# Values loaded between head pairs 1 and 2 in the first unit of a sparse attention and gated FFN kernel

## The chip, the core and the metric

The kernel runs on one core of a Trainium2 chip. The metric is the device time of one execution in microseconds; lower is better. The engines are named as in the profile: PE is TensorE (matmuls), PEld its weight loads, DVE is VectorE, ACT is ScalarE, POOL is GpSimd, and SP is SyncE, which here only issues DMAs. PSUM is the memory that PE writes[...].

## What is computed

The attention sees, for each query, a band of nearby keys (a distance below 16) and one entry for each block of 32 keys: the elementwise maximum of the block's keys, and the mean of its values. A gated FFN with a residual follows. Cut to what matters, the reference is:

```python
B, H, S, D = q.shape                         # 4, 8, 768, 64
block, window = (32, 16)
k_sum = k.reshape(B, H, nb, block, D).max(axis=3)
v_sum = v.reshape(B, H, nb, block, D).mean(axis=3)
scores_l = scale * np.matmul(q, k.transpose(0, 1, 3, 2))
mask_l = np.abs(pos[:, None] - pos[None, :]) < window
scores_s = scale * np.einsum('bhsd,bhnd->bhsn', q, k_sum) + np.log(block)
a = softmax(concat([where(mask_l, scores_l, -1e9), scores_s]))
attn = a @ concat([v, v_sum])                # then (B*S, H*D) = (3072, 512)

g = x @ w_gate                               # 512 x 1536
gelu = 0.5 * g * (1.0 + erf(g * inv_sqrt2))
ffn_out = gelu * (x @ w_val) @ w_out         # 1536 x 512
res_gate = 1.0 / (1.0 + np.exp(-(x @ w_res)))
return x + res_gate * ffn_out
```

## The kernel before

**Tiling.** The work is cut into 8 units (`NU`): unit u is half (384 queries, `TU`) of batch u // 2. Inside a unit the heads go in four pairs (`NP`), two heads of 64 dimensions filling 128 partitions. The queries are taken in tiles of 64 (`QT`). For each tile, `kW` holds 128 key columns: 96 of the band (the tile's own 64 and 16 on either side) and 24 block maxima, the rest zero. So one matmul (`s_step`, L330) gives both kinds of score. ACT takes the exponential into `P` (L336, L339). `av_part` multiplies `P` by `vext`, which holds the band's values in rows 0 to 95, and by the block means in rows 96 to 127, which for unit 0 come from a tile of their own, `vsum`. A column of ones gives the softmax's denominator. `av_norm` divides (L370, L372), and `xt_step` transposes the result into `xT` (L381 on PE, L383 on ACT).

**The FFN.** For each of 12 column groups of 128 (`FO`), `fo_step` multiplies `xT` by `w_gate` and by `w_val`, four matmuls each over the head pairs (`half_fo`, L398). ACT applies Gelu and DVE the product. `ffn_step` multiplies by `w_out` (L432), `res_step` by `w_res`, and `end_step` stores.

**What sets the order.** There is one order, written out by hand (`tc.manual_schedule()`): each engine runs its instructions in the order in which the code names them. Buffers come from pools, and an instruction waits until its inputs are there and its buffer is free. In PSUM, `MM` has four banks that are handed out in turn, `AO` and `TT` one bank each, and `SS` two.

**The loads.** All the casting loads are issued by POOL in one queue: first k and q of head pair 1 (heads 2, 3; `load_tokens`, L91), then those of pairs 2 and 3, then the values (`load_values`, L100; seven transfers, of which c = 6 and c = 0 come first), then the weights in six column slices, with the second half of q (`qb`) ahead of the last slice, `w_res` and `w_out`. k and q of pair 0 come as fp32 through SP. Between these issues POOL builds constants with `select` (L119): the identity `ident`, the mask `maskt`, the bias, and `bmean`, the matrix with 1/32 in each block's place that sums values to block means on PE.

**The first unit**, before the loop over units, goes:
- `k_first(hp)`: 16 transposes of k on PE (L226), and ACT's copy into `kW` (L228); `k_first_rest`: DVE's block maximum from the same PSUM tile (L234) and three copies (L236 to L238); `q_step`: the same for q (L195, L219).
- For each pair `mask_into` writes the mask into PSUM ahead of the scores (L313), so that the scores need no mask after it. `s_step` follows.
- `vsum_sum` (L279) sums the value blocks over seven matmuls into `vs`; `vsum_out` (L284) copies them to `vsum`. `v_spread` (L291, L294) copies values inside `vext` for the odd tiles.
- `av_part` runs in two halves: `blocks=False` for the band, `blocks=True` for the block means.
- `keep_warm(n)` issues n matmuls on a constant tile (L449). A Gelu on one element (L504) brings the Gelu table load ahead of the FFN.
- `firsts` holds the four PSUM tiles of FFN columns 0 and 1, into which each pair's projection goes as soon as its `xT` is there.

In the order before, all four pairs' scores are issued ahead of the band part of `av_part`. The second half's q, `qb`, is transposed inside unit 0's FFN loop (L596 to L598), behind columns 9 and 10; after the loop come the next unit's scores, `s_step(n, 0)` and `s_step(n, 1)`, the latter writing to `AO` and `TT`.

Of the kernel before, what the change touches and what calls it, by code (L numbers as in the profile page):

```python
# [8 lines left out]
F32 = mybir.dt.float32  # L9
BF16 = mybir.dt.bfloat16  # L10
AF = mybir.ActivationFunctionType
ALU = mybir.AluOpType
# [3 lines left out]
def kernel(  # L16
# [11 lines left out]
    nc = tc.nc  # L28
    B, H, S, D = q.shape
    assert (B, H, S, D) == (4, 8, 768, 64)  # L30
    BLK, WIN = 32, 16
# [57 lines left out]
    def load_tokens(t, src, b, lo, hi, h0, h1):  # L89
        j = (hi - lo) // PP  # L90
        nc.gpsimd.dma_start(  # L91
            out=t[:, h0:h1].rearrange("p h j d -> p h (j d)"),
            in_=src[b, h0:h1, lo:hi].rearrange("h (p j) d -> p h (j d)", j=j),
        )
# [9 lines left out]
    with tc.manual_schedule():  # L104
# [13 lines left out]
        def select(ap, op, fill, base, step, cm):  # L118
            nc.gpsimd.affine_select(out=ap, in_=ap, compare_op=op, fill=fill, base=base,  # L119
                                    pattern=[[step, ap.shape[-1]]], channel_multiplier=cm)  # L120

        nc.vector.memset(warm[:], 0.0)
        nc.vector.memset(ident[:], 0.0)
        nc.vector.memset(bias_t[:], 0.0)
        nc.vector.memset(bias_t[96:128, :], logblk)
        nc.vector.memset(bmean[:], 1.0 / BLK)
        nc.vector.memset(maskt[:], 1.0)
        vext_consts(0)
        kw_consts(0)
        nc.vector.memset(vsum[0][96:128, :, D:D + 1], 1.0)  # L130
# [7 lines left out]
        load_tokens(kt, k, 0, 0, S, 2, 4)  # L138
        select(ident[:], ALU.not_equal, 1.0, 0, -1, 1)
        load_tokens(qa, q, 0, 0, TU, 2, 4)  # L140
        for h in (4, 6):
            load_tokens(kt, k, 0, 0, S, h, h + 2)
            load_tokens(qa, q, 0, 0, TU, h, h + 2)
        select(maskt[0:96], ALU.is_ge, 0.0, -1, -1, 1)
        select(maskt[0:96], ALU.is_ge, 0.0, 2 * WIN - 1, 1, -1)
        load_values(0, NC)
# [1 line left out]
        select(bias_t[96:128, :], ALU.is_ge, -30000.0, NB - 1, 0, -1)  # L148
        for c in range(1, NC):
            load_values(0, c)  # L150
        select(bmean[:], ALU.is_ge, 0.0, 32 * (NB + 94) - WIN, -32, 1)
        select(bmean[:], ALU.is_ge, 0.0, 31 + WIN - 32 * (NB + 94), 32, -1)

        wg_src = moe_w_gate.rearrange("(ko ki) f -> ki ko f", ki=128)
        wv_src = moe_w_val.rearrange("(ko ki) f -> ki ko f", ki=128)
        for c in range(6):
            sl = slice(c * 256, (c + 1) * 256)
            if c == 5:
                load_tokens(qb, q, 0, TU, S, 0, H)
            nc.gpsimd.dma_start(out=w_gate[:, :, sl], in_=wg_src[:, :, sl])  # L160
            nc.gpsimd.dma_start(out=w_val[:, :, sl], in_=wv_src[:, :, sl])
        nc.gpsimd.dma_start(out=w_res[:], in_=moe_w_res.rearrange("(ko ki) f -> ki ko f", ki=128))
        wo_src = moe_w_out.rearrange("(fo ki) f -> ki fo f", ki=128)
        for c in range(3):
# [52 lines left out]
        def q_step(src, b, lo, hi, hp, pool, tag, copy=nc.scalar.copy):  # L217
            tp = turn_pair(src, hp, pool, tag)
            copy(qT[b % 2][hp][:, lo:hi].rearrange("d (p j) -> d p j", j=tp.shape[2]), tp)  # L219
# [12 lines left out]
        def k_first_rest(tp, kw):  # L232
            ks = work.tile([128, NB], BF16, tag="ks", name="ks")
            nc.vector.tensor_reduce(out=ks[:], in_=tp.rearrange("d j (n w) -> d n j w", w=4),  # L234
                                    axis=mybir.AxisListType.XY, op=ALU.max)
            nc.vector.tensor_copy(kw[:, 0:HT, BLK0:BLK0 + NB], ks.unsqueeze(1).to_broadcast([128, HT, NB]))  # L236
            nc.vector.tensor_copy(kw[:, 1:HT, 0:WIN], kw[:, 0:HT - 1, OWN + QT - WIN:OWN + QT])
            nc.vector.tensor_copy(kw[:, 0:HT, POST:POST + WIN], kw[:, 1:HT + 1, OWN:OWN + WIN])  # L238
# [44 lines left out]
        def vsum_out(b, vs, h0, h1, copy):  # L283
            copy(vsum[b % 2][96:128, h0:h1, 0:D],  # L284
                 vs[96:128, h0 * D:h1 * D].rearrange("p (h d) -> p h d", d=D))

        def v_spread(b, c0, c1, part):

# [190 lines left out]
        k_first_rest(*t)  # L479
        t = k_first(1)  # L480
        q_step(qa, 0, 0, TU, 1, *MM)
        k_first_rest(*t)
        s = mask_into(s_tiles())
        keep_warm(2, s1[0])
        s_step(0, 0, st, s)
        keep_warm(2, s1[0])
        mask_into(s1)
        t = k_first(2)
        q_step(qa, 0, 0, TU, 2, *MM)
        k_first_rest(*t)  # L490
        s_step(0, 1, st, s1, True)
        s = mask_into(s_tiles())
        t = k_first(3)
        q_step(qa, 0, 0, TU, 3, *MM, nc.vector.tensor_copy)
        k_first_rest(*t)
        vs = ps_mm.tile([128, DM], F32, tag="mm", name="vs")
        keep_warm(1, vs)
        s_step(0, 2, st, s)
        s3 = mask_into(s_tiles((AO, TT)))
        wp = ps_mm.tile([128, 512], F32, tag="mm", name="wp")  # L500
        vsum_sum(0, *MM, (NC, 0), vs)
        keep_warm(2, wp)
        s_step(0, 3, st, s3, True)
        nc.scalar.activation(pre[:], bias_t[0:1, :], AF.Gelu)  # L504
        v_spread(0, 0, HT // 2, 0)
        v_spread(0, 0, HT // 2, 1)
        vsum_sum(0, *MM, (1, 2, 3), vs, first=False)
        keep_warm(2, wp)
        homes = (MM, MM, AO, TT)
        for hp in range(2):  # L510
            av_part(0, hp, st, *homes[hp], blocks=False)
        vsum_sum(0, *MM, (4,), vs, first=False)
        for hp in range(2, NP):
            av_part(0, hp, st, *homes[hp], blocks=False)
        keep_warm(1, wp)
        vsum_sum(0, *MM, (5,), vs, first=False, last=True)
        keep_warm(1, wp)
        vsum_out(0, vs, 0, 2, nc.vector.tensor_copy)
        vsum_out(0, vs, 2, 8, nc.scalar.copy)
        for hp in range(NP):  # L520
            av_part(0, hp, st, blocks=True)
            av_norm(hp, st)
        two = ps_s.tile([128, 2, 512], F32, tag="s", name="gv0")
        firsts = [(w_gate, 0, two[:, 0, :]), (w_val, 0, two[:, 1, :]), (w_gate, 1, None), (w_val, 1, None)]
        for hp in range(NP):
            xt_step(0, hp, st, *(MM, MM, AO, TT)[hp], nc.scalar.copy)
            if hp == 0:
                keep_warm(2, wp)
            if hp:
                firsts = [(w, fo, half_fo(st, w, fo, hp - 1, hp, acc)) for w, fo, acc in firsts]  # L530

        for u in range(NU):
            b, half = u // 2, u % 2
# [16 lines left out]
            for fo in range(FO):  # L550
                if u == 0 and fo < 2:
                    for w, _, acc in firsts[2 * fo:2 * fo + 2]:
                        half_fo(st, w, fo, KO - 1, KO, acc)
                    fo_end(gvT, fo, firsts[2 * fo][2], firsts[2 * fo + 1][2])
                elif u > 3 and fo == 0:
                    fo_end(gvT, fo, firsts[0][2], firsts[1][2])
                elif u > 3 and fo == 1:
                    fo_end(gvT, fo, firsts[2][2], half_fo(st, w_val, fo, 0, KO))
                else:
                    fo_step(st, gvT, fo)  # L560
                values_step(u, fo)
                if u == 0 and fo == 4:
                    nc.vector.memset(vsT[:], 0.0)
                    load_rows(1)
                if u == 0 and fo == 6:
                    vext_consts(1)
                if u == 0 and fo == FO - 1:
                    kw_consts(1)
                    for c in range(NC + 1):
                        load_values(1, c)  # L570
                if u == 2 and fo == FO - 1:
                    gate(gvT[0:1, fo, 0:1])
                    load_rows(3)
                if half == 0 and 1 < nb < B and fo == 0:
                    vT[nb] = turn_values(nb)
                    turn_batch(nb, 0, NP - 1)
                if half == 1 and 1 < nb < B and fo == 0:
                    turn_sums()
                    turn_batch(nb, NP - 1, NP)
                if half == 1 and 1 < nb < B and fo in (0, 2, 4, 11):  # L580
                    k_rest(kW[nb % 2][(0, 2, 4, 11).index(fo)])
                if u == 1 and fo == 6:
                    gate(gvT[0:1, fo, 0:1])
                    load_batch(2)
                if u == 1 and fo in (1, 2, 6, 7):
                    home = TT if fo % 2 else AO
                    if fo < 4:
                        k_step(nb, fo - 1, *home)
                    else:
                        q_step(q_sb[nb], nb, 0, S, fo - 6, *home)  # L590
                if u == 1 and fo == FO - 1:
                    k_rest(kW[1][2])
                    k_rest(kW[1][3])
                if u == 0 and fo >= FO - 4:
                    k_later(kW[0][fo - FO + 4])
                if u == 0 and fo in (FO - 3, FO - 2):  # L596
                    for hp in range(2 * (fo - FO + 3), 2 * (fo - FO + 3) + 2):
                        q_step(qb, 0, TU, S, hp, *(TT if hp % 2 else AO))  # L598
            nst = new_unit() if n < NU else None
            if u == 0:  # L600
# [118 lines left out]
```

The softmax here doesn't subtract the row's maximum and nothing guards it: scores larger than these inputs give would overflow.

## Time and profile before

| | |
|---|---|
| median of 3 runs | 259.57 us (258.91 to 259.62) |
| the profiled execution's own time | 259.77 us |
| its span | 257.9 us |
| PE busy | 250.2 us, 97% |
| DVE, ACT, POOL busy | 69%, 50%, 39% |
| granted PE clock | 1.00 |
| moved by DMA | 30.16 MB, of it 19.11 MB through POOL's queue |

The span is the time from the first to the last instruction of the program in one profiled execution; some 2 us of the execution's own time lie around it. In the profile a row of the timeline gives start, length, engine, line, operation, what is written and read, and in brackets how long the engine had been idle before it and what released it. A DMA's row gives the time that the issuing engine spent on it; its landing is given apart, counted from the issue.

### The profile page before, as it was taken

Reading aid. Unit: us, or ns where it says so; the run is one execution under the profiler, and the core shown is the slowest. Engines: PE = TensorE matmul, PEld = TensorE weight load, DVE = VectorE, ACT = ScalarE, POOL = GpSimd, SP = SyncE. Lnnn points to the kernel's source line nnn. Section 1 sums busy time; section 2 is a strip of 40 time slices with the busy share of each in tenths; the row PEclk is TensorE's granted clock in tenths of the full one; section 3 lists DMA queues with packets and bytes.
Section 4 is the critical chain, followed back from the end, with each engine's and each line's share of the span. In section 5 each row is a group of like instructions: output and inputs, shape, how many; then the busy total and the mean of one; then the engine's idle time right before and its main releaser. Section 6 shows DMA issues by size and latency. Waiting matters only on the chain.

```text
span 257.9 us, 5755 instructions
## 1 busy us (share of the span) xinstructions
PE 250.2 (97%) x2249; PEld 139.5 (54%) x2249; DVE 178.3 (69%) x426; ACT 129.5 (50%) x223; POOL 101.0 (39%) x139
## 2 busy tenths in 40 slices
PE   7989999999999999999999999999999999999993
PEld 3546555566545555555554565555554665556543
DVE  5756866595598878679959768679768853764333
ACT  4855369455635637553373537453473537443310
POOL 7995542795699910996650100020001000010000
PEclk9999999999999999999999999999999999999999
DMA  7999999999999999999994995165003200130012
GB/s 157 151 151 193 199 202 199 142 209 123 151 152 165 179 129 167 125 186 202 154 134 90 146 145 103 31 153 68 1 3 86 84 0 0 33 137 3 1 41 83
DMA packets 117899, 30.16 MB, mean 117 GB/s; under 512 B 104816, under 2 KB 115504, under 8 KB 117872
## 3 DMA queue, kind: packets, MB, share of 16 engines
q0 software_dynamic: 86640, 19.11, 86.7%
q1 hardware_dynamic: 31232, 10.69, 25.6%
q8 instruction: 17, 0.28, 0.5%
q14 instruction: 10, 0.08, 0.1%
HBM read 32.51 MB, written 6.29 MB: 150 GB/s over the span
## 4 chain that ended last, share of the span: by engine, by line
PE 79%; DVE 7%; DMA 5%; POOL 4%; issue 2%; ACT 1%; POOLq 0%; DVEq 0%
PE f L432 22%; PE vv L398 19%; PE g L398 18%; PE r L416 8%; PE ao L362 3%; DMA k_sb<-in_k_dram 3%; PE gv L548 3%; DMA vext<-in_v_dram 2%; PE s L330 2%; DVE gvT L405 2%; PE xp L381 1%; POOL k_sb L175 1%; POOL vext L100 1%; DVE ks L211 1%; DVE vext L294 1%
## 5 line engine op out<-in xcount | busy, mean ns | idle before, releaser
L398 PE MATMUL vv<-xT,w_val 128*128 128x384 bf16 x364 | 74.5, 326 | 0.1
L404 ACT ACTIVATE ge<-g 128x384 f32<-128x384 f32 x87 | 42.7, 491 | 63.3 <-PE g L398 37.0
L398 PE MATMUL g<-xT,w_gate 128*128 128x384 bf16 x348 | 71.3, 326 | 0.4 <-DVE gvT L405 0.2
L405 DVE TENSOR_TENSOR gvT<-ge,vv 128x384 bf16<-128x384 f32 x91 | 50.0, 553 | 27.5 <-PE vv L398 25.5
L432 PE MATMUL f<-w_out,gvT 128*128 128x512 bf16 (+2 forms) x312 | 68.4, 363 | 0.0
L398 PEld LDWEIGHTS <-w_val 128*128 128x128 bf16 x368 | 36.0, 98 | 24.0 <-issue 0.4
L398 PEld LDWEIGHTS <-w_gate 128*128 128x128 bf16 x352 | 34.1, 98 | 23.2 <-issue 1.1
L432 PEld LDWEIGHTS <-gvT 128*128 128x128 bf16 x312 | 28.3, 98 | 28.2
L443 POOL DMA_DIRECT2D out_dram<-o x12 | 6.5, 544 | 90.9 <-DVE rz L370 76.0
L422 ACT ACTIVATE th<-r 128x512 f32<-128x512 f32 x24 | 14.2, 602 | 24.8 <-PE r L416 24.8
L437 DVE SCALAR_TENSOR_TENSOR th<-th,f 128x512 f32<-128x512 f32 (+2 forms) x26 | 16.7, 642 | 12.3 <-PE f L432 8.5
L175 POOL DMA_DIRECT2D k_sb<-in_k_dram x24 | 19.8, 839 | 12.5 <-DMA w_out<-in_moe_w_out_dram 5.2
L416 PE MATMUL r<-w_res,xT 128*128 128x512 bf16 x96 | 24.4, 380 | 0.0
L100 POOL DMA_DIRECT2D vext<-in_v_dram x28 | 23.2, 875 | 1.5 <-PE g L398 1.2
L175 POOL DMA_DIRECT2D q_sb<-in_q_dram x24 | 20.0, 875 | 1.6 <-DMA k_sb<-in_k_dram 1.4
L347 DVE TENSOR_TENSOR P<-P,maskt 128x768 bf16<-128x768 bf16 x28 | 15.3, 556 | 7.2 <-ACT P L336 3.9
L372 DVE TENSOR_TENSOR xn<-ao,rz 128x384 bf16<-128x384 f32 x32 | 17.8, 558 | 1.1
L383 ACT COPY xT<-xp 128x384 bf16<-128x384 bf16 x20 | 9.3, 482 | 16.5 <-PE xp L381 14.8
L439 DVE SCALAR_TENSOR_TENSOR o<-th,xn 128x512 f32<-128x512 f32 (+2 forms) x26 | 16.9, 651 | 0.9
L336 ACT ACTIVATE P<-s,bias_t 128x384 bf16<-128x384 f32 x32 | 16.8, 579 | 1.3 <-PE s L330 1.3
L339 ACT ACTIVATE P<-s,bias_t 128x768 bf16<-128x768 f32 x16 | 14.5, 904 | 3.5 <-PE s L330 3.4
L175 POOL DMA_DIRECT2D v_sb<-in_v_dram x16 | 13.2, 850 | 2.8 <-DMA q_sb<-in_q_dram 2.5
(99 smaller groups left out, 236.0 us busy)
## 6 DMA issues: line engine op xcount, KB each, us to landing
out_dram<-o POOLq DMA_DIRECT2D x12, 256.0 KB, 2.4
out_dram<-o SPq DMA_DIRECT2D x11, 256.0 KB, 4.2
vext<-in_v_dram POOLq DMA_DIRECT2D x20, 128.0 KB, 7.4
k_sb<-in_k_dram POOLq DMA_DIRECT2D x24, 96.0 KB, 7.7
q_sb<-in_q_dram POOLq DMA_DIRECT2D x24, 96.0 KB, 5.5
w_gate<-in_moe_w_gate_dram POOLq DMA_DIRECT2D x6, 256.0 KB, 8.5
w_val<-in_moe_w_val_dram POOLq DMA_DIRECT2D x6, 256.0 KB, 9.1
w_out<-in_moe_w_out_dram POOLq DMA_DIRECT2D x3, 512.0 KB, 14.9
```

The source lines that it names most:

```text
L100: nc.gpsimd.dma_start(out=dst, in_=v[b, :, lo:hi, :].rearrange("h p d -> p h d"))
L175: nc.gpsimd.dma_start(out=sb[b][:, h // 2, :, h % 2 * D:h % 2 * D + D], in_=src[b, h].rearrange("(c p) d -> p c d", c=NC))
L336: nc.scalar.activation(P[:, hh].rearrange("p t q -> p (t q)"), s[hh][:, 0:TU], AF.Exp, scale=scale, bias=bias_t[:])
L347: nc.vector.tensor_mul(Pf, Pf, maskt.unsqueeze(1).to_broadcast([128, 2 * HT, QT]))
L372: nc.vector.tensor_mul(xn, ao[:, :, :, 0:D], rz.to_broadcast([128, NSUB, 2, D]))
L398: nc.tensor.matmul(acc[:, 0:TU], w[:, ko, fs], st["xT"][:, ko, :], start=(ko == 0), stop=(ko == KO - 1))
L404: nc.scalar.activation(ge[:], g[:, 0:TU], AF.Gelu)
L405: nc.vector.tensor_mul(gvT[:, fo, :], ge[:], vv[:, 0:TU])
L416: nc.tensor.matmul(r[:], st["xT"][:, ko, ss], w_res[:, ko, :], start=(ko == 0), stop=(ko == KO - 1))
L432: nc.tensor.matmul(st["f", sub][:, 0:c1 - c0], gvT[:, fo, ss], w_out[:, fo, c0:c1], start=(fo == 0), stop=(fo == FO - 1))
L437: nc.vector.scalar_tensor_tensor(th, th, 1.0, f[:, 0:c1 - c0], ALU.add, ALU.mult)
L439: nc.vector.scalar_tensor_tensor(o[:, 0:c1 - c0].rearrange("p (k d) -> p k d", d=128), th.rearrange("p (k d) -> p k d", d=128), 0.5, st["x ...
```

## The change

In unit 0's loads, the transfers of k and q of head pairs 2 and 3 go behind all the values instead of ahead of them. The order of the work follows: behind pair 1's scores come the block sums, their copy and the `av_part` of pairs 0 and 1, and only then pair 2 and after it pair 3, each with its transposes, scores, exponential and `av_part`. Pair 0's and 1's normalisation, transposes and projections are put in between. `bmean` is no longer made by two `select` calls on POOL but by DVE, out of the identity, in a new function `block_means` (three reductions and a scaling), called ahead of pair 1's block maximum. `vsum_out` is done by ACT alone. The load of `qb` is cut into two halves of four heads, one ahead of the last weight slice and one behind it; the transposes of its second half go from behind column 10 to behind column 11. The number of `keep_warm` matmuls in the front goes from 23 to 24.

```diff
-        nc.vector.memset(bmean[:], 1.0 / BLK)
-        nc.vector.memset(maskt[:], 1.0)
+        nc.vector.memset(bmean[:], 0.0)      # and maskt's memset two lines up
...
         load_tokens(qa, q, 0, 0, TU, 2, 4)
-        for h in (4, 6):
-            load_tokens(kt, k, 0, 0, S, h, h + 2)
-            load_tokens(qa, q, 0, 0, TU, h, h + 2)
         select(maskt[0:96], ALU.is_ge, 0.0, -1, -1, 1)
         select(maskt[0:96], ALU.is_ge, 0.0, 2 * WIN - 1, 1, -1)
         load_values(0, NC)
...
         for c in range(1, NC):
             load_values(0, c)
-        select(bmean[:], ALU.is_ge, 0.0, 32 * (NB + 94) - WIN, -32, 1)
-        select(bmean[:], ALU.is_ge, 0.0, 31 + WIN - 32 * (NB + 94), 32, -1)
+        for h in (4, 6):
+            load_tokens(kt, k, 0, 0, S, h, h + 2)
+            load_tokens(qa, q, 0, 0, TU, h, h + 2)
...
             if c == 5:
-                load_tokens(qb, q, 0, TU, S, 0, H)
+                load_tokens(qb, q, 0, TU, S, 0, 4)
             nc.gpsimd.dma_start(out=w_gate[:, :, sl], in_=wg_src[:, :, sl])
             nc.gpsimd.dma_start(out=w_val[:, :, sl], in_=wv_src[:, :, sl])
+        load_tokens(qb, q, 0, TU, S, 4, H)
...
+        def block_means():
+            c = NB + 93
+            with nc.allow_low_precision("sums of one element"):
+                for lo, hi, x in ((0, WIN, c), (WIN, 128 - WIN, c + 1), (128 - WIN, 128, c + 4)):
+                    n = (hi - lo + BLK - 1) // BLK
+                    nc.vector.tensor_reduce(out=bmean[:, x:x + n],
+                                            in_=ident[:, lo:hi].rearrange("p (n w) -> p n w", n=n),
+                                            axis=mybir.AxisListType.X, op=ALU.add)
+            nc.vector.tensor_scalar_mul(bmean[:, c:c + 5], bmean[:, c:c + 5], 1.0 / BLK)
...
         q_step(qa, 0, 0, TU, 1, *MM)
+        block_means()
         k_first_rest(*t)
...
         mask_into(s1)
+        s_step(0, 1, st, s1, True)
+        vs = ps_mm.tile([128, DM], F32, tag="mm", name="vs")
+        wp = ps_mm.tile([128, 512], F32, tag="mm", name="wp")
+        keep_warm(2, wp)
+        vsum_sum(0, *MM, (NC, 0), vs)
+        keep_warm(2, wp)
+        for c in range(1, NC):
+            vsum_sum(0, *MM, (c,), vs, first=False, last=c == NC - 1)
+            keep_warm(1, wp)
+        v_spread(0, 0, HT // 2, 0)
+        v_spread(0, 0, HT // 2, 1)
+        vsum_out(0, vs, 0, H, nc.scalar.copy)
+        av_part(0, 0, st, *AO, blocks=False)
+        av_part(0, 1, st, *TT, blocks=False)
+        keep_warm(1, wp)
         t = k_first(2)
         q_step(qa, 0, 0, TU, 2, *MM)
         k_first_rest(*t)
+        av_part(0, 0, st, blocks=True)
+        av_part(0, 1, st, blocks=True)
         s = mask_into(s_tiles())
+        s_step(0, 2, st, s)
+        av_norm(0, st)
+        q_step(qa, 0, 0, TU, 3, *MM, nc.vector.tensor_copy)
         t = k_first(3)
         k_first_rest(*t)
+        xt_step(0, 0, st, *AO, nc.scalar.copy)
+        av_part(0, 2, st, *MM, blocks=False)
+        av_part(0, 2, st, blocks=True)
+        s = mask_into(s_tiles())
+        s_step(0, 3, st, s)
         nc.scalar.activation(pre[:], bias_t[0:1, :], AF.Gelu)
+        av_norm(1, st)
+        xt_step(0, 1, st, *TT, nc.scalar.copy)
+        av_norm(2, st)
+        av_part(0, 3, st, *MM, blocks=False)
+        av_part(0, 3, st, blocks=True)
+        av_norm(3, st)
...
+        firsts = [(w, fo, half_fo(st, w, fo, 0, 1, acc)) for w, fo, acc in firsts]
+        for hp in range(2, NP):
+            xt_step(0, hp, st, *(AO, TT)[hp % 2], nc.scalar.copy)
+            for w, fo, acc in firsts:
+                half_fo(st, w, fo, hp - 1, hp, acc)
...
-                if u == 0 and fo in (FO - 3, FO - 2):
-                    for hp in range(2 * (fo - FO + 3), 2 * (fo - FO + 3) + 2):
+                if u == 0 and fo in (FO - 3, FO - 1):
+                    for hp in ((0, 1) if fo == FO - 3 else (2, 3)):
                         q_step(qb, 0, TU, S, hp, *(TT if hp % 2 else AO))
```

More of the change, by code (lines that the diff above doesn't have):

```diff
@@ L123 @@
         nc.vector.memset(ident[:], 0.0)
+        nc.vector.memset(maskt[:], 1.0)
         nc.vector.memset(bias_t[:], 0.0)
         nc.vector.memset(bias_t[96:128, :], logblk)
-        nc.vector.memset(bmean[:], 1.0 / BLK)
-        nc.vector.memset(maskt[:], 1.0)
+        nc.vector.memset(bmean[:], 0.0)
         vext_consts(0)
@@ L490 @@
         k_first_rest(*t)
-        s_step(0, 1, st, s1, True)
+        av_part(0, 0, st, blocks=True)
+        av_part(0, 1, st, blocks=True)
         s = mask_into(s_tiles())
+        s_step(0, 2, st, s)
+        av_norm(0, st)
+        q_step(qa, 0, 0, TU, 3, *MM, nc.vector.tensor_copy)
         t = k_first(3)
-        q_step(qa, 0, 0, TU, 3, *MM, nc.vector.tensor_copy)
         k_first_rest(*t)
-        vs = ps_mm.tile([128, DM], F32, tag="mm", name="vs")
-        keep_warm(1, vs)
-        s_step(0, 2, st, s)
@@ L499 @@
[L499 to L522, printed above, removed]
+        xt_step(0, 0, st, *AO, nc.scalar.copy)
@@ L523 @@
+        av_part(0, 2, st, *MM, blocks=False)
+        av_part(0, 2, st, blocks=True)
+        s = mask_into(s_tiles())
+        s_step(0, 3, st, s)
+        nc.scalar.activation(pre[:], bias_t[0:1, :], AF.Gelu)
+        av_norm(1, st)
[4 more added lines that the diff above has]
+        av_norm(3, st)
         two = ps_s.tile([128, 2, 512], F32, tag="s", name="gv0")
         firsts = [(w_gate, 0, two[:, 0, :]), (w_val, 0, two[:, 1, :]), (w_gate, 1, None), (w_val, 1, None)]
[L525 to L530, printed above, removed]
+        firsts = [(w, fo, half_fo(st, w, fo, 0, 1, acc)) for w, fo, acc in firsts]
```

## The prediction

> **What bounds the kernel now.** I read the page's busy line and slices first (PE 97%, clock 9 in every slice), then the waits of PE, to see where it is not busy. Over 24 us to the end the view of PE's waits has one line:
>
> ```profile
> PE g L398 <- DVE gvT L405: 0.2, 1, 0.2
> ```
>
> So from 24 us on TensorE is the bound and stands still 0.2 us in 234 us. Whatever the front (0 to 24 us, where unit 0's attention is built up) gains or loses is passed on one to one, unless a weight transfer then becomes late. The chain of waits over the front says what the front waits for (start, length, what):
>
> ```profile
> 9.55 5.97 DMA vext<-in_v_dram
> 15.52 0.04 issue
> 15.56 0.38 PE vs L279
> ...
> 18.75 0.48 ACT vsum L284
> ...
> 24.11 0.65 PE g L398 x4
> ```
>
> The values do it: the chain lies on a value load until 15.52, then on the block sums, their copy to `vsum`, the normalised heads, the transposes, the first projections. I call 24.11 **the mark**: unit 0's first two FFN columns are done and PE runs full from there. The last value load:
>
> ```profile
> L100 POOL DMA_DIRECT2D vext<-in_v_dram x1: 923/923/923, 11.3 to 11.3; - x1
> ...
> DMA to landing us min/median/max: 6.1/6.1/6.1
> ```
>
> It is issued at 11.31 and lands at 17.4; the mark comes 6.7 us after that. Those 6.7 us are so few because all four head pairs' scores and exponentials are finished by then (last exponential 16.04). What a head pair costs is shown by pair 2 in the timeline (start, length; idle before it in brackets):
>
> ```profile
> 10.08 0.80 ACT L228 COPY kW<-tp 128x768 bf16<-128x768 bf16 x1 [0.36 <-PE tp L226]
> 10.91 0.96 DVE L234 TENSOR_REDUCE ks<-tp 128x24 bf16<-128x768 bf16 x1 [1.26 <-ACT kW L228]
> 12.11 0.17 DVE L238 COPY kW<-kW 128x96 bf16<-128x96 bf16 x1
> 12.34 0.35 PE L330 MATMUL s<-qT,kW 64*128 64x64 bf16 x12 [0.47 <-DVE kW L238]
> 12.76 0.94 ACT L339 ACTIVATE P<-s,bias_t 128x768 bf16<-128x768 f32 x1
> 16.06 1.28 ACT L504 ACT_TABLE_LOAD   x1
> 17.36 0.20 ACT L504 ACTIVATE pre<-bias_t 1x1 f32<-1x1 f32 x1
> ```
>
> The reader is to see a serial relay ACT, DVE, PE, ACT: copy 0.80, then the block maximum and copies 1.43 (10.91 to 12.34), then 0.42 to the exponential, then 0.9. The Gelu table load lies in a time when ACT has nothing to do.
>
> [...] each L234 starts 0.03 to 0.08 us after the ACT copy of the same `tp` ends, so these two add up. [...] The trace's PE starts follow the program. [...] `pre` starts 0.02 later. I use 1.50 for load and `pre`.
>
> **The change part by part.**
>
> *Loads.* The four issues of k and qa for pairs 2, 3 (heads 4 to 7) cost POOL 3.19 to 5.68, 2.5 us. Moved behind the values, they let every value load be issued 2.5 earlier: the last at 8.8, landing at 14.9 with the same 6.1. With less queued ahead, latency could fall to the 5.2 of the first large value load, giving 14.2. I take 14.9. Call it L. The four land after L: about 0.6 apart by their issues (9.8, 10.4, 11.1, 11.7) with 5 to 6 us, so 15.2 to 17.7. POOL no longer runs the two `bmean` selects (12.26 to 12.89), so weights start 0.63 earlier; SP holds only kf and qf here and is passed by nothing.
>
> *Block means on DVE.* Three reductions and one scaling. The L234 row (768 elements, 0.955) and the L211 row (384, 0.553) give about 0.15 + 1.05 ns an element: 0.17, 0.25, 0.17, and at most 0.17 for the scaling, 0.76 in all; 0.45 if they overlap as the copies do (starts 0.1 apart). They stand ahead of pair 1's reduction, so pair 1's scores move from 10.14 to at most 10.5. The work behind it (sums) waits for values: its PE work without waits ends near 13.8, before L. Cost 0 below that cover, at most 0.4 if L were 13.5. The memset swaps cost nothing: as many of the same size.
>
> *The order on PE.* This is the cost. The last sum matmul waits for L, and everything of pairs 2, 3 stands behind it on PE. From L, with the rows above:
> - last sum and a warm matmul 0.45; pairs 0, 1 window part, 24 matmuls 0.55; warm 0.2: L+1.2
> - pair 2: transposes to ACT copy 0.58, copy 0.83, maximum and copies 1.43, scores 0.42: exponential at L+4.45, done L+5.4
> - pair 3: its `kW` copy stands behind that exponential on ACT: 0.8, then 1.45, 0.42 and 0.92: done at L+9.0
> - Gelu load and `pre`, now ahead of pair 1's `xT` copy on ACT: 1.5, L+10.5; `xT` copy 0.48: L+11.0
> - projections with xT 1, the transposes of pair 3, projections with xT 2 and 3: 0.65 + 0.2 + 0.65 + 0.65: L+13.15.
>
> Av parts 2 and 3, `v_spread`, `vsum_out`, the norms and projections with xT 0 are hidden beside the ACT and DVE steps; if ACT or DVE were faster, they (0.6 to 0.8 each) would be next. The new mark is 14.9 + 13.15 = 28.05: **+3.9** (28.05 − 24.11). With L = 14.2 it is +3.2.
>
> *Weights.* The last FFN slice (w_val) was issued at 24.02, landed 11.3 later, 35.3, and was used at 35.57. After, transfers land 0.63 earlier or more and PE needs them 4 us later: no wait. Cost 0.
>
> *qb in halves.* One issue more, 0.8 us on POOL, which here idles about 0.6 before each issue until an older transfer lands: hidden, bounds 0 and +0.1. The q_steps of pairs 2, 3 go from behind column 10 to behind column 11, straight ahead of `s_step(1, 1)`, which writes the banks AO and TT that they occupy. Before, ACT's copies of a pair of q_steps ended 1.26 us after the transposes began (36.31 to 37.57) under column 11's matmuls. Now only pair 0's scores lie between (PE 0.53 + 0.25), so PE stands about **0.5**. ACT's table load starts 0.8 later, but 3.5 us of residual and FFN matmuls cover it. Bounds 0.2 and 0.9; nothing excludes a smaller wait, a gain is excluded since the same matmuls run.
>
> Sum: +3.9 + 0.5 = +4.4 on the profiled execution, whose span is 257.9 and time 259.77: 264.2. The median of the runs is 259.57, 0.2 below: I forecast 264.0.
>
> **Rivals.**
> - *Faster: the values' earlier landing pays in full.* If the 6.7 us from last value to mark stayed, the mark would be 21.6. Then the transfers bind: w_res lands at 37.8 (25.31 + 12.5), 37.2 after, against a use at 38.63, so 1.4 of the 2.5 could be kept; less 0.5 for the q_steps, −0.9: 258.7. It is decided where pair 3's scores start. From there 5.5 us remain to the mark (0.42 + 0.92 + 1.5 + 0.48 + 2.15), so a tie needs them at 18.1; I place them at 22.55. Against it: the PE order, and two relays through ACT and DVE that the trace prices at 3.6 each.
> - *Half the loss.* Latency down to 5.2, the q_step wait at 0.2, and the Gelu load started under pair 3's norm: 3.2 + 0.2 − 0.7 = +2.7, 262.3.
> - *The PE clock drops.* From 18 to 26 us I leave PE idle 3.5 of 8 us, against 0.31 before (busy 7.69). The gaps are 1.2 at most[...]. If a window were half speed nonetheless, about 2.2 us of dense projections would double: 266.2.
> - *Pairs 2, 3 land late* (after L+4.9 = 19.8 for pair 3, two us later than I place it): each us adds one, 265 or more.
> - *It does not do what it says*, the loads being held elsewhere: the slots of k and qa are their own and the queue keeps program order, so hardly any chance.
>
> **How the numbers follow.** About 0.3% (0.8 us) is what a measurement of this kernel can tell from no change. Forecast 0.70 (263.2 to 264.9), half the loss 0.12, clock drop or late pairs 0.13, faster 0.03, near zero by overlaps I missed 0.02. The range takes in the half loss and most of the slow cases: 262.0 to 266.5.
>
> **What would show it.** Right: the last value landing near 14.9; pair 2's L228 near 16.7, pair 3's near 20.4; L504's table load near 24 between an exponential and an `xT` copy that waits for it; PE's waits of about 1 us before each L330 of pairs 2 and 3; full PE from about 28; a wait near 0.5 in front of `s_step(1, 1)`. Wrong: a mark ahead of 25, or pair 3's scores ahead of 19; then the relay is not serial. A larger loss with PE matmuls at double length would be the clock.

## The result, and the profile after

| | before | after |
|---|---|---|
| median of 4 runs | 259.37 us (258.91 to 259.62) | 269.13 us (268.22 to 269.80) |
| ratio after to before | | 1.0376 (95%: 1.034 to 1.0413) |
| profiled execution, its span | 259.77 us, 257.9 us | 269.80 us, 268.0 us |
| granted PE clock, mean | 1.00 | 0.978 |

The change costs 9.8 us by the medians and 10.1 us between the two profiled executions. The forecast was 264.0, with a range to 266.5: the direction was right, and less than half of the loss was foreseen. The ratios in this document leave disturbed runs out, which matters for e1_warm (one of four) and e8_cold (eight of twelve) alone: their runs spread by 2 and 3%, and their profiles fell on their longest run.

The chain of waits over the first 32 us of the kernel after (start, length, what) answers to the chain of before:

```profile
15.24 0.22 PE vs L278
...
17.00 0.81 ACT kW L227
17.83 0.97 DVE ks L233
...
19.35 0.36 PE s L340 x12
19.74 0.90 ACT P L349
20.64 0.70 ACT kW L227
21.36 0.97 DVE ks L233
...
22.88 0.52 PE s L340 x12
23.42 0.91 ACT P L349
24.37 1.01 PE ao L372 x19
25.38 0.75 PE gv L408 x2
...
28.37 0.32 PE xp L391 x3
28.69 0.64 PE gv L408 x2
...
31.20 0.65 PE g L408 x4
```

The last block sum (`vs`) is done early, as the loads promised. Behind it stands the relay that the prediction described: copy of `kW`, maximum, scores, exponential, once for pair 2 (17.00 to 20.64) and once for pair 3 (20.64 to 24.33). So far it is on the forecast's times. Then comes what was not foreseen: from 24.37 PE alone is on the chain, and it takes until 31.20 for the mark, where 28.05 was forecast. The lengths show why: `xp` x3 takes 0.32, a pair of projections 0.64. Before the change the same work took half as long:

```profile
21.75 0.17 PE xp L381 x3
21.92 0.33 PE gv L398 x2
```

The view of stretches of time gives the clock beside PE's busy time (start:end, length, busy of PE, PEld, DVE, ACT, POOL, then the granted PE clock, DMA share, GB/s):

```profile
17.40:20.80 3.40, 2.02 (x62) 1.33 (x57) 2.55 (x7) 1.84 (x4) 2.48 (x4) 1.00 1.44 193
20.00:24.00 4.00, 3.33 (x60) 1.87 (x54) 3.09 (x9) 2.29 (x4) 2.16 (x3) 0.60 1.46 199
24.00:28.00 4.00, 3.63 (x35) 2.31 (x36) 0.87 (x3) 2.64 (x5) 2.17 (x3) 0.50 1.45 194
28.00:32.00 4.00, 4.00 (x19) 2.12 (x17) 0.79 (x2) 1.47 (x4) 1.67 (x3) 0.62 1.45 196
```

Between 17.4 and 20.8 PE was busy 2.02 of 3.40 us. At 20.8 the clock fell to half, and it came back at 31.0, 10.2 us later. The dense projections, which could have caught up, ran at half speed.

The waits of PE from 14 us to the end (how long in all, how often, the longest):

```profile
PE s L340 <- DVE rz L380: 1.8, 2, 1.3
PE ao L372 <- DVE vext L310: 1.6, 2, 1.2
PE xp L391 <- DVE xn L382: 0.9, 1, 0.9
PE g L408 <- DVE gvT L415: 0.5, 1, 0.5
...
PE s L340 <- ACT qT L218: 0.2, 1, 0.2
```

The first line is the relay's two waits and the last the q_steps'. The second and the third have no counterpart in the kernel before, and lie at 84 to 89 us, in unit 1, far from anything that the change touches. The timeline there, DVE and PE first, then POOL:

```profile
84.71 3.11 DVE L310 COPY vext<-vsum 32x768 bf16<-32x768 bf16 x4
...
85.42 0.38 PE L372 MATMUL ao<-vext,P 128*64 128x65 bf16 x12 [1.18 <-DVE vext L310]
86.24 0.38 PE L372 MATMUL ao<-vext,P 128*64 128x65 bf16 x12 [0.44 <-DVE vext L310]
...
83.38 6.71 POOL L174 DMA_DIRECT2D v_sb<-in_v_dram  x8
```

The same four copies in the kernel before, and what POOL did beside them:

```profile
76.26 1.49 DVE L300 COPY vext<-vsum 32x768 bf16<-32x768 bf16 x4
...
76.30 2.67 POOL L175 DMA_DIRECT2D q_sb<-in_q_dram  x3 [0.41 <-DMA k_sb<-in_k_dram]
```

These copies put unit 1's block means into `vext`, and PE's `av_part` waits for them. Before, they took 1.49 us together and PE did not wait. After, they take 3.11 us beside an unbroken row of DMA issues on POOL, and one copy ends per issue (0.82 us). Before, POOL had just been held up by a transfer for 0.41 us when they began. But before, too, POOL issued beside all four. How long each copy took there (shortest, median, longest in ns):

```profile
L300 DVE COPY vext<-vsum x4: 348/362/660, 76.3 to 77.4; 32x768 bf16<-32x768 bf16 x4
```

Three of the four took 0.35 to 0.37 us; they ended within 0.6 us of the start of an issue (76.30 and 77.30). Only the third, which began half way through the first issue, took 0.66 and ended 0.16 us behind that issue's end. After the change all four end 0.19 to 0.20 us behind the end of an issue (85.37, 86.18, 87.00 and 87.82 against 85.17, 85.99, 86.81 and 87.63). So what tells the long copies from the short isn't POOL's issuing as such, but where in an issue a copy falls: in the unbroken row each copy met the late part of one.

Laid side by side by landmarks, the 10.1 us are these (the row of `g` x4 that begins the mark stands at 23.95 before and 31.03 after in the timeline; r is the row of the residual's matmuls, L416 before and L426 after):

| stretch | before | after | cost |
|---|---|---|---|
| start to the mark's row | 23.95 | 31.03 | 7.08 |
| mark's row to r of unit 0 | 14.68 | 15.24 | 0.56 |
| r of unit 0 to the second r row of unit 1 | 35.64 | 35.64 | 0.00 |
| from there to the third r row | 5.34 | 7.78 | 2.44 |
| from there to the end of the span | 178.3 | 178.3 | 0.0 |

### The profile page after: what moved, and what is told of

The parts are those of the page before. It is cut to its first block, busy times and chain, and to the rows that moved or that the text cites. A ratio compares the mean times of both kernels' runs of the same rounds, so it can differ in the third digit from the quotient of the medians.

```text
span 268.0 us, 5735 instructions
## 1 busy us (share of the span) xinstructions
PE 254.5 (95%) x2226; PEld 142.4 (53%) x2250; DVE 180.6 (67%) x429; ACT 129.6 (48%) x222; POOL 101.3 (38%) x138
## 4 chain that ended last, share of the span: by engine, by line
PE 84%; DVE 9%; issue 2%; ACT 2%; DMA 1%; DVEq 0%
PE f L442 21%; PE vv L408 20%; PE g L408 20%; PE r L426 7%; PE ao L372 3%; PE gv L561 3%; PE s L340 3%; DMA kf<-in_k_dram 1%; PE xp L391 1%; DVE gvT L415 1%; DVE vext L310 1%; DVE ks L210 1%; PE gv L408 1%; DVE vext L304 1%; PE tp L225 1%
## 5 line engine op out<-in xcount | busy, mean ns | idle before, releaser
L408 PE MATMUL vv<-xT,w_val 128*128 128x384 bf16 x364 | 75.3, 328 | 0.0
L408 PE MATMUL g<-xT,w_gate 128*128 128x384 bf16 x348 | 72.1, 328 | 0.8 <-DVE gvT L415 0.5
L442 PE MATMUL f<-w_out,gvT 128*128 128x512 bf16 (+2 forms) x298 | 66.5, 362 | 0.8 <-issue 0.2
L442 PEld LDWEIGHTS <-gvT 128*128 128x128 bf16 x312 | 28.3, 98 | 28.3
L447 DVE SCALAR_TENSOR_TENSOR th<-th,f 128x512 f32<-128x512 f32 (+2 forms) x26 | 16.7, 641 | 12.3 <-PE f L442 8.5
L100 POOL DMA_DIRECT2D vext<-in_v_dram x28 | 23.8, 931 | 3.0 <-PE g L408 1.9
L426 PE MATMUL r<-w_res,xT 128*128 128x512 bf16 x88 | 24.0, 380 | 0.4
L174 POOL DMA_DIRECT2D k_sb<-in_k_dram x24 | 19.7, 844 | 8.9 <-DMA w_out<-in_moe_w_out_dram 5.5
L349 ACT ACTIVATE P<-s,bias_t 128x768 bf16<-128x768 f32 x17 | 15.3, 901 | 9.0 <-PE s L340 8.9
L346 ACT ACTIVATE P<-s,bias_t 128x384 bf16<-128x384 f32 x30 | 15.7, 578 | 0.2 <-PE s L340 0.2
L372 PEld LDWEIGHTS <-P 128*64 128x64 bf16 (+2 forms) x432 | 9.3, 114 | 9.2 <-issue 4.5
## 6 DMA issues: line engine op xcount, KB each, us to landing
w_out<-in_moe_w_out_dram POOLq DMA_DIRECT2D x3, 512.0 KB, 13.7
```

The lines of the kernel that those rows point to most:

```text
L100: nc.gpsimd.dma_start(out=dst, in_=v[b, :, lo:hi, :].rearrange("h p d -> p h d"))
L174: nc.gpsimd.dma_start(out=sb[b][:, h // 2, :, h % 2 * D:h % 2 * D + D], in_=src[b, h].rearrange("(c p) d -> p c d", c=NC))
L346: nc.scalar.activation(P[:, hh].rearrange("p t q -> p (t q)"), s[hh][:, 0:TU], AF.Exp, scale=scale, bias=bias_t[:])
L372: nc.tensor.matmul(ao[64 * e:64 * e + 64, sub, hh, :], P[rows, hh, t, :], rhs, start=blocks is None or (not blocks and sub == 0 and hh == ...
L408: nc.tensor.matmul(acc[:, 0:TU], w[:, ko, fs], st["xT"][:, ko, :], start=(ko == 0), stop=(ko == KO - 1))
L426: nc.tensor.matmul(r[:], st["xT"][:, ko, ss], w_res[:, ko, :], start=(ko == 0), stop=(ko == KO - 1))
```

## The experiments

**The first four** undo the suspected costs one at a time and then together. In e1_warm matmuls on a constant tile fill PE's two waits:

```diff
+        keep_warm(5, wp)
         s_step(0, 2, st, s)
...
-        s = mask_into(s_tiles())
+        s = s_tiles()
+        keep_warm(4, s[:, 0])
+        mask_into(s)
         s_step(0, 3, st, s)
```

> The changed kernel with nine more keep_warm matmuls in the relay: five ahead of pair 2's scores, four ahead of pair 3's mask. Theory 'clock': PE is granted half clock from 20.6 us on because the relay leaves it too idle; filled, the clock stays at 1.00, the projections run at 0.16 us apart again, the mark (full PE) comes near 28.2 and not 31.1, and the time falls by 2.5 to 3.2 us to about 266.3. Rival 'relay alone': the projections wait for ACT's xT copies behind the Gelu load in any case, so the clock costs under 0.7 us and the time stays above 268.3. Second rival: nine matmuls of 0.22 us stand in PE's way and cost up to 2 us.

Measured: 264.16 to 269.18 us in four runs, ratio 1.0236 (1.0176 to 1.0296). In the profiled execution the front kept the full clock, and the mark's row stands at 27.99, r of unit 0 at 43.23, 3.04 earlier than after. Unit 1's stall remained, and in this execution, the longest, the clock fell there (0.72 between 80 and 90 us); the mean clock of the other three was 0.993 to 1.00, so that this second drop is not the rule.

e2_qsteps loads `qb` whole again and puts its transposes back behind column 10:

```diff
-                load_tokens(qb, q, 0, TU, S, 0, 4)
+                load_tokens(qb, q, 0, TU, S, 0, H)
...
-        load_tokens(qb, q, 0, TU, S, 4, H)
...
-                if u == 0 and fo in (FO - 3, FO - 1):
+                if u == 0 and fo in (FO - 3, FO - 2):
```

> The changed kernel with qb loaded whole ahead of the last weight slice and all its transposes behind columns 9 and 10, as before. Theory: PE's stand in front of s_step(1, 1) (its start to the residual matmuls takes 0.66 us more than before) goes, and with it 0.5 to 0.7 us: about 268.5. Rival: what follows has slack of its own and the time stays within 0.2 us; or the whole qb makes the last weight slice late, and it is not faster at all.

Measured: 267.79 us, ratio 1.0292 (1.0266 to 1.0318). From the mark's row (30.00) to r of unit 0 (44.69) it takes 14.69, as before the change (14.68); after, 15.24. So the q_steps' place is worth 0.55. In the profiled executions the half clock was also shorter here (21.5 to 28.3 us): from the last block sum (15.52) to the mark's row it takes 14.48, after 15.96. That doesn't explain why the median fell by 1.3 and not by 0.55: two of the six runs have mean clocks like the lowest of after's (0.978 and 0.979), and took 267.72 and 268.16, about as long as the others. It may be scatter, and stays open.

e3_gate holds back the issues of v for batch 2, by a one-element copy on POOL that waits for unit 1's block means:

```diff
-                    load_batch(2)
+                    load_rows(2, 0, 2)          # k and q alone
...
                     vsum_bc(1, hp, 0, HT)
+                gate(vext[1][96:97, 0, H - 1, 0:1])
+                load_rows(2, 2, 3)
+                for c in range(NC + 1):
+                    load_values(2, c)
```

> The changed kernel with the loads of batch 2's value rows (v_sb and the values after them) held back on POOL, by a one-element copy, until unit 1's four copies of the block means (vsum_bc on DVE) are done. Theory[...]: those copies take 0.66 to 0.90 us each and not 0.36 because POOL is issuing DMAs through all of them; held back, they take about 0.36 each, PE's waits on them (1.6 us) and on the norm behind them (0.9) go, and the time falls by 2.0 to 2.5 us to about 266.9. Rival 'late inputs': the copies come late because vsum or the spread comes late, and the time stays. Second rival: the value rows now come late for unit 2 and give the gain back.

Measured: 266.84 us, ratio 1.0247 (1.0212 to 1.0282). The view of this tile's copies on DVE (shortest, median, longest in ns), after and then e3_gate:

```profile
L310 DVE COPY vext<-vsum x4: 659/900/900, 84.7 to 86.9; 32x768 bf16<-32x768 bf16 x4
```

```profile
L310 DVE COPY vext<-vsum x7: 356/364/366, 84.1 to 99.0; 32x768 bf16<-32x768 bf16 x7
```

With POOL still, a copy takes 0.36 us, and the stretch between unit 1's second and third r row falls from 7.78 to 5.90 (81.33 to 87.23). The front is as after: from the last block sum (14.51) to the mark's row (30.45) 15.94 us, after 15.96.

e4_all is the three edits together, so what it keeps is the relay and the moved loads alone:

> The three edits together. If the causes are separate, the sum of the three: 269.1 - 2.8 - 0.65 - 2.3 = about 263.4, that is +4.0 on the kernel before, the relay's part of the prediction (+3.9) alone. If the late stall in unit 1 depends on when unit 1 comes, the parts overlap and it stays above 264.5; if the relay was mis-sized, its mark is off 28.1 in the trace.

Measured: 263.63 us (263.26 to 264.77), ratio 1.0139 (1.0104 to 1.0174), span 261.8. From the page, the clock in 40 slices:

```profile
PEclk9999999999999999999999999999999999999999
```

and from the timeline the last block sum and the mark's row:

```profile
14.43 0.38 PE L277 MATMUL vs<-vext,bmean 128*128 128x512 bf16 x1 [0.53 <-DMA vext<-in_v_dram]
...
27.95 0.81 PE L407 MATMUL g<-xT,w_gate 128*128 128x384 bf16 x4
```

The mark's row stands at 27.95, +4.00 on before, where the prediction had +3.9 for the relay. From the last sum to it 13.52 us, in e1_warm 13.35, against 15.96 and 15.94 with the clock at half: **the clock costs 2.5 us** in the profiled execution. It is no accident of one execution that it was lost: the mean clock is 0.978 to 0.987 in all four runs of after, and 1.00 in all four of e4_all.

**Is it the order or the loads?** e5_loads keeps the order of work of before and moves the loads alone (`block_means` goes with it); e6_order has the new order and the loads of before:

```diff
# e5_loads, against before
-        for h in (4, 6):
-            load_tokens(kt, k, 0, 0, S, h, h + 2)
-            load_tokens(qa, q, 0, 0, TU, h, h + 2)
...
         for c in range(1, NC):
             load_values(0, c)
+        for h in (4, 6):
+            load_tokens(kt, k, 0, 0, S, h, h + 2)
+            load_tokens(qa, q, 0, 0, TU, h, h + 2)
```

> The kernel before with its own order of work and only the loads of the change: k and q of pairs 2, 3 behind the values, the block-mean constant made by DVE. Theory 'the relay is the price': whichever order the work has, pairs 2 and 3 now start at their landings (about 15 to 17.6 us, not 8 to 10.9), two runs of transposes, copy, maximum, scores and exponential follow, and the mark comes 4.5 to 7 us late: 264 to 267. Rival 'only PE's order costs', as the prediction put it: with the order of before, the loads alone cost under 2 us, below 262.

> The changed kernel with its order of work, but the loads of pairs 2, 3 ahead of the values as before. Theory: pair 2's transposes stand in PE's program behind the last value's sum whatever has landed; that value lands 2.5 us later, so everything from there on is 2 to 2.5 us later than in the changed kernel: about 271.3. Rival: the pairs' early landing pays, because the relay was waiting for their transfers, and the time is the changed kernel's or better (269 or less).

e5_loads: 270.5 us, ratio 1.0404 (1.0369 to 1.044). Its waits of PE have

```profile
PE tp L224 <- DMA k<-in_k_dram: 4.9, 1, 4.9
```

and the clock fell to half in that wait as well (12.8 to 19.7 us). Its profile is of its fastest run, 267.23 us. e6_order: 272.7 us, ratio 1.0466 (1.042 to 1.0512); its last block sum runs at 17.07, 2.0 later than after, and the mark's row at 32.65, with the clock at half from 21.8 to 32.0. So neither part is the one that costs: e5_loads can't be told from after, and e6_order loses more. What they share is that the relay of pairs 2 and 3 starts only behind what lands last, in e5_loads because their own k lands last, in e6_order and after because PE's order puts them behind the values. At full clock neither was tried, so how much of their loss is the relay's alone is not known.

**The rest of unit 1's stall.** e7_gate_all is e4_all with all of batch 2's loads held, not v alone:

```diff
                 if u == 1 and fo == 6:
-                    gate(gvT[0:1, fo, 0:1])
-                    load_rows(2, 0, 2)
+                    pass
...
                 gate(vext[1][96:97, 0, H - 1, 0:1])
-                load_rows(2, 2, 3)
-                for c in range(NC + 1):
-                    load_values(2, c)
+                load_batch(2)
```

> As e4_all (warm matmuls added, q_steps back), but all of batch 2's loads (k, q, v rows and values) are held on POOL until unit 1's block-mean copies are done, not the value part alone. Theory[...]: what was left of the stall in unit 1 in e4_all (the residual matmuls of sub-tiles 1 to 2 lie 5.90 us apart against 5.34 before) comes from POOL issuing k and q rows beside DVE's earlier copies, so it goes: 5.3 us and about 263.1. Rival: the rest is PE's own order, and nothing changes. Second rival: the late loads hold up unit 2 or 3 and the time rises.

Measured: 276.26 us, ratio 1.0614 (1.0553 to 1.0674). The stretch in unit 1 falls to 4.86 (81.14 to 86.00), below the 5.34 of before. So POOL's issues cost unit 1 up to 2.92 us after and 0.48 before; e3_gate, which holds v alone, leaves 1.04. But the loads are then late for the next units, and PE's waits, at 106 and 117 us, show the bill:

```profile
PE vv L407 <- DVE gvT L414: 3.7, 1, 3.7
PE ao L371 <- DVE P L356: 3.4, 1, 3.4
```

Just behind each of these waits the clock fell to half for 3.4 us, and once in the front too (18.2 to 21.6). Here the last value also landed at 16.3, two us later than in e4_all (14.4), with nothing changed ahead of it: between these two executions the landing differs by that much.

**Is it the lateness or the change's own code?** e11_late is the kernel before with 19 more warm matmuls ahead of the mark, some 4.1 us; e12_late_gate adds e3_gate's hold:

```diff
             if hp == 0:
-                keep_warm(2, wp)
+                keep_warm(21, wp)
```

> The kernel before with 19 more warm matmuls (19 x 0.216 = 4.1 us) in one place of the front, behind pair 0's transposes: the same work, made 4.1 us late with PE busy. Theory 'late front': unit 1's block-mean copies now meet POOL's unbroken DMA issues, take up to 0.9 us each, and the time rises by 4.1 + 2.4 = 6.5 us. Rival 'the stall belongs to the change's code': it rises by 4.1 us alone, and the residual matmuls of unit 1's sub-tiles 1 and 2 stay 5.3 us apart.

> e11_late with the value rows of batch 2 held on POOL until the block-mean copies are done. Theory[...]: copies of about 0.36 us, the 5.34 us between unit 1's residual matmuls up to 5.9 at most, and 1.5 to 2.4 us less than e11_late. Rival: no change against e11_late, if something else in the late unit 1 makes the copies slow.

e11_late: 268.2 us, ratio 1.0305 (1.0253 to 1.0357). e12_late_gate: 265.9 us, ratio 1.0236 (1.0186 to 1.0287). The copies in e11_late and then in e12_late_gate:

```profile
L300 DVE COPY vext<-vsum x4: 659/898/899, 82.5 to 84.7; 32x768 bf16<-32x768 bf16 x4
```

```profile
L300 DVE COPY vext<-vsum x4: 356/356/367, 80.8 to 81.6; 32x768 bf16<-32x768 bf16 x4
```

Nothing of the change is in e11_late, and it has the same long copies; the stretch from second to third r row is 8.62 there (with the clock at half from 84.8 to 88.2) and 5.91 with the hold. The mark's row stands at 29.28 in e11_late's profile, 5.3 later than before, and at 27.57 in e12_late_gate's, 3.6 later. In both profiles 8.8 us lie behind the start of the last output matmuls, against 7.0 before, since DVE waits 1.8 and 2.0 us there for a store of the output; the comparison of the two is free of it. So some four microseconds lost ahead of unit 1 bring this stall without the change. The likely reason, read from POOL's rows and not tried by itself: before, its issues for batch 2 have pauses in which it waits for transfers still on their way (1.13, 0.89 and 0.41 us, ahead of the issues at 68.39, 70.10 and 76.30); when PE, which opens their gate, comes 4 us later, it finds none to wait for and issues without a pause (from 68.17 in e11_late and 70.40 after).

**What the clock costs, from the other side.** e9_nowarm is e4_all without the nine warm matmuls of e1_warm:

```diff
-        keep_warm(5, wp)
         s_step(0, 2, st, s)
...
-        keep_warm(4, s[:, 0])
```

> e4_all without its nine added warm matmuls: the q_steps back, the value rows held, the relay as idle as in the changed kernel. Theory 'clock': the granted clock falls to 0.5 in the relay again and the time is 2.0 to 3.2 us above e4_all, near 266.5 where before has 260. Rival 'the warm matmuls are worth nothing by themselves': within 0.5 us of e4_all.

Measured: 264.82 us (264.65 to 265.44), ratio 1.0188 (1.0149 to 1.0228). In its view of stretches PE's busy share falls as after, and so does the clock:

```profile
20.00:24.00 4.00, 2.53 (x44) 1.33 (x43) 3.01 (x9) 2.06 (x4) 2.29 (x3) 0.64 1.45 197
24.00:28.00 4.00, 3.76 (x35) 2.31 (x36) 0.75 (x2) 2.51 (x5) 2.22 (x3) 0.50 1.46 195
```

From the last block sum (14.72) to the mark's row (29.56) it takes 14.84, 1.3 more than in e4_all, and the medians differ by 1.2: both less than I expected. The clock was at half for 6.8 us here (21.2 to 28.0) and 10.2 after, so the price depends on when the full clock comes back: 1.0 in e2_qsteps, 1.3 here, 2.5 after and in e3_gate.

e8_cold is the kernel before without the 13 warm matmuls that follow pair 0's and 1's transposes:

> The kernel before without the 13 warm matmuls that stand behind the first k transposes; all the real work is left. Theory 'clock by share of busy time': with gaps of PE of about 1 us at most, but PE busy perhaps half of the time between 8 and 18 us, the granted clock falls to 0.5 for some 3.4 or 10 us[...], and the time rises by 1.5 to 4 us. Rival[...]: it stays at 1.00, and the time is the same or up to 0.5 us shorter.

Measured: 259.77 to 268.09 us in twelve runs, ratio 1.0028 (0.9986 to 1.007). The profiled one, the longest, has the clock at 0.50 between 16 and 24 us and r of unit 0 at 42.11. The runs are too far apart to say what the warm matmuls of before are worth in time, and I rest no price on them. But the mean clock is 0.964 to 0.996 in the twelve runs and 0.996 to 1.000 in the fifteen of before beside them, and in the profiled one it fell at 15.2 us with no gap of PE longer than 1.05 us ahead of the fall. So here the order of before, too, lost the clock with no gap longer than that.

**Was the Gelu table load on the path?** e10_pre is e4_all with it behind the last `xT` copy:

```diff
         s_step(0, 3, st, s)
-        nc.scalar.activation(pre[:], bias_t[0:1, :], AF.Gelu)
...
                 half_fo(st, w, fo, hp - 1, hp, acc)
+        nc.scalar.activation(pre[:], bias_t[0:1, :], AF.Gelu)
```

> e4_all with the one-element Gelu, and so the Gelu table load, behind the last xT copy instead of ahead of pair 1's. The prediction put its 1.5 us on the path in full: then the mark comes 1.5 us earlier. Theory from e4_all's trace: behind the load PE waits only 0.26 us for pair 1's xT, since pair 3's av_part and the projections with xT 0 keep it until then, so the mark moves by 0.3 us and the time by 0 to 0.3 us. Third: the load now holds up the first Gelu of the FFN and gives it all back.

Measured: 264.24 us, ratio 1.0162 (1.012 to 1.0203), which can't be told from e4_all's. From the last block sum (14.29) to the mark's row (27.52) it takes 13.23 us, 0.29 less than in e4_all, but from there to r of unit 0 it takes 15.37 and not 14.68: PE loses 0.31 us ahead of the row of `g` x4 at 29.13 and 0.23 ahead of that at 30.66. I put that down to the first Gelu, which now comes behind the table load; it was not measured by itself.

## Why the prediction was wrong

**The loads: right.** The last value was issued at 9.2 (forecast 8.8) and landed 5.3 later, near 14.5 (14.9). That brought nothing, since the relay stands behind it. The weights began 0.2 us earlier and not 0.63, at no cost.

**The relay: right in its steps, and in part lucky in its sum.** Pair 2's `kW` copy 17.00 (forecast 16.7), pair 3's 20.54 (20.4), the table load at 24.33 (near 24), the `xT` copy of pair 1 at 25.74 (L+11.0 = 25.9). At full clock its whole cost is the +4.00 of e4_all, against +3.9. But in e4_all the last value landed at 14.4, 0.5 us ahead of the forecast's L, and the relay took 13.7 us from there to the mark (28.11), where 13.15 was forecast; the two misses cancel. The 0.6 us came in small pieces: pair 2's exponential began at L+4.8 (4.45), pair 3's ended at L+9.4 (9.0), and from pair 1's `xT` copy to the mark it took 2.4 (2.15). The table load was on the path: with `pre` it took 1.50 us (23.85 to 25.35). That taking it off gained 0.29 alone (e10_pre) means that a second path, PE's own work, ended only 0.29 us sooner; a sum along one path doesn't show that.

**The attribution "The order on PE. This is the cost": too narrow.** e5_loads has the old order and loses no less, its half clock included.

**The q_steps: right.** +0.56, forecast 0.5.

**The clock: the step that failed first.** I gave half clock a place among the cases that share 0.13, with the sentence that the gaps are "1.2 at most". The gaps were indeed 1.29 at most, and the clock fell all the same, with PE busy 59% of the 3.4 us before. That gaps so short would keep the clock was an assumption of mine, which the trace of before, with none above 0.47 us from 4 us on, could not test; this run decides against it. I had the sign in hand: 3.5 of 8 us idle against 0.31 before. The size I gave that rival, 2.2 us, was near the 2.5 measured; the likelihood was wrong. That the thin PE of the relay is the cause is shown by e4_all against e9_nowarm, which differ in the nine warm matmuls alone: PE is busy 3.02 of 3.40 us between 16.0 and 19.4 with them, and keeps the full clock; without them it is busy 2.04 in that stretch, and the clock falls at 21.2. No border can be read from these traces, however. e4_all kept the clock through a stretch of 2.29 of 3.40 us (20.6 to 24.0), but e2_qsteps ran one of 1.55 of 3.40 (13.6 to 17.0, with a gap of 1.59) at full clock and lost it only at 21.5. The half clock lasted 10.2 us after, in e3_gate and in e6_order, 6.8 in e2_qsteps and e9_nowarm, 6.9 in e5_loads, and 3.4 in unit 1 of e11_late and at each of three places in e7_gate_all; what sets these lengths, and why one thin stretch lost the clock and another did not, is not shown here.

**"Whatever the front gains or loses is passed on one to one, unless a weight transfer becomes late": the step that failed second.** The exception was too narrow. I looked for what the delay makes late, and asked nothing of what it makes *coincide*. POOL's loads for batch 2 are paced partly by DMA (its pauses of 0.41 to 1.13 us before) and DVE's copies by PE, so 4 us of delay shifted one against the other, worth +2.44, about the size of the clock's part. The copies took 0.36 us with POOL still, and 0.66 to 0.90 where each ended just behind a DMA issue; but before the change three copies took 0.35 to 0.37 in the first 0.6 us of an issue, so an issue didn't slow them over its whole length. That taking the issues away takes the stall away is shown by e3_gate (the stretch in unit 1 5.90 us against 7.78), e12_late_gate (5.91 against 8.62) and e7_gate_all (4.86 against 5.34 before), the first two with copies of 0.36 us; what in an issue on POOL lengthens a copy on DVE is not shown here.

**What is left.** 0.6 us of the front's +7.08 belongs to the profiled execution: its first scores ran at 10.31 where e3_gate and e4_all have theirs at 8.36 and 8.45, and its last block sum ran 0.6 later than theirs. PE was slow for longer at the start, as the same two warm matmuls show, after and then before:

```profile
6.63 1.03 PE L459 MATMUL s<-warm 128*128 128x512 bf16 x2
```

```profile
6.18 0.60 PE L449 MATMUL s<-warm 128*128 128x512 bf16 x2
```

(The granted clock of the views doesn't show this: the trace's record of it begins at 10.5 us in this execution, at 6.2 before.) e11_late's profile has the same late start (9.7 us). So the sum against the profiled execution is 259.77 + 4.0 (relay) + 2.5 (clock) + 0.6 (late start) + 0.56 (q_steps) + 2.44 (unit 1) = 269.9, against 269.80. From after to e4_all the span falls by 6.2; clock, start, q_steps and unit 1 (1.88 of it) account for 5.5, and the other 0.7 lies behind unit 1; its cause is open.

## What to carry to other kernels

The serial relay over several engines cost twice here: its own waits (+4.00 us), and then the dense work behind it, at half clock, 2.5 us more. So count PE's busy share over stretches of a few us (2.02 of 3.40 ahead of the fall), not only its longest gap (1.29), and price a case in which what follows runs at half speed for some us (3.4 to 10.2 in these runs). When a delay is to be passed on "one to one", ask what each queue that is not paced by the bound engine will be doing at the new moment: here DVE's copies met the late part of DMA issues on POOL, at 0.66 to 0.90 us each and not 0.36, once the one had moved against the other. And when a load is moved ahead, follow what now lands last and how long its own chain is, whichever group that is.

## What the runs showed of the hardware that I had not expected

- Half clock without a long gap: longest 1.29 us, PE busy 2.02 of 3.40 us, then 10.2 us at 0.50 although PE was busy 3.63 to 4.00 of every 4 us for the last seven of them. It lasted 3.4 us each time in e7_gate_all, 6.8 in e9_nowarm and 10.2 in e3_gate.
- DVE's small copies between SBUF tiles (32x768, bf16) took 0.36 us beside a still POOL (e3_gate, e12_late_gate), and also where they ended within the first 0.6 us of a DMA issue on POOL (three copies before the change). After, beside issues without a pause (0.82 each), they took 0.66 to 0.90, and each ended 0.2 us behind an issue.
- The same value load, with the same transfers ahead of it, landed at 14.4 us in e4_all and 16.3 in e7_gate_all.
